# Half of w2 in parts for the second group's later experts, and attention units that share their TensorE stretches

## The chip, the cores and the metric

The kernel runs on one core of one Trainium2 chip. The metric is the device time of one execution in microseconds, as the median over several runs; lower is better. Before the change it is 1072.7 us (three runs, 1072.57 to 1072.9).

## The reference

An attention block feeds a mixture of experts. B=4 batches, H=8 heads, S=768 positions, D=48 per head; then N=3072 rows of 384 features, E=4 experts, F=1024 hidden units, all in float32.

```python
for t in range(S):                      # gated linear attention, recurrent form
    state = alpha[:, :, t, :, None] * state + einsum('bhd,bhe->bhde', k[:, :, t], v[:, :, t])
    y[:, :, t] = einsum('bhd,bhde->bhe', q[:, :, t], state)
x = y.transpose(0, 2, 1, 3).reshape(B * S, H * D)
p = domain_probs / (domain_probs.sum(-1, keepdims=True) + 1e-09)
for e in range(E):
    h = maximum(x @ w1[e], 0.0)
    out += p[:, e:e + 1] * (h @ w2[e])
```

## The kernel before

**Attention in units.** The sequence is cut into chunks of 128 positions, 6 chunks for each of 4 batches. That makes 24 units, numbered `u`, chunk by chunk; unit `u` works on all 8 heads of one batch and one chunk. `attention(u)` is a generator with 17 steps:

- Steps 0 to 2 transpose alpha, keys and queries on TensorE (`tp`) and ask for the next unit's alpha, keys and queries from memory.
- The chunk is treated in 7 levels of doubling block length. Each level copies a part of the queries (`copy_q`, ScalarE, tile `qb`), multiplies the queries with decays (`next_q`, VectorE) and the keys too (`next_k`, both). Each level needs the one before it. Steps 3 to 6 are levels 0 to 2 and the query copy of level 3.
- Step 7 multiplies queries and keys for levels 0 to 3 on TensorE (`products`, tile `sc`, 64 records) and merges them under masks (`take`). Steps 8, 9 and 10 are levels 4, 5 and 6.
- Step 11 is `far` (the last level) and the products of levels 4 and 5 (`sc`, 32 records). Steps 12 and 13 copy the scores to the tile `lat`, step 14 transposes the keys back.
- Step 15 is `result()`: it multiplies scores with values and queries with the state (tile `yps`). Step 16 is the state update: a product of keys and values (tile `sps`), two VectorE operations for each half of the state, and the loads of the values of unit `u + 2`. Of the product `sps` only the blocks of a head with itself are used.

**Experts in groups.** The 24 units are put in 7 groups: the first of 2 units, five of 4, the last of 2. A group of 4 gives 512 rows of x. A task is one group with one expert; the last two groups share each expert's weights. `up(gi, e, fc)` computes one of 8 row tiles of h (128 hidden units x 512 rows) into the PSUM tiles `one` and `two`; `down(gi, e, slots, between)` multiplies h with w2 for one or two of the group's units into `ops`, and `add_up` adds that to the accumulator `acc`, weighted by the expert's probability.

**Products in parts.** A float32 product on TensorE can be done plainly, or as three products of the type float32r with operands split into `top`, `low` and a correction `dif`. `split1(gi, e)` and `split2(gi, e)` say which task has w1 or w2 in parts: w1 from the second group on, w2 from the third. In parts, h is split too (`hidden_parts`: a ScalarE relu, a VectorE operation for `low`, two half-width ones for `dif`); plainly, it is a relu in place (`rectified`). The `up` sets VectorE `t<-t,two` or `hT<-t,two` accordingly.

**Splitting the weights.** The first group splits w1 and the second group splits w2, each weight in 16 pieces (4 per expert). `split_piece` takes two ScalarE operations and two VectorE operations per piece, in steps that `background()` runs between other work, and a GpSimd DMA writes the split piece to a buffer in memory (`kept`), from where later groups load it (SyncE queue). The second group's raw w2 piece is loaded into a part of the h tile that is free, and `down` uses it plainly from there.

**Who sets the order.** Everything is put out in an order written by hand: `advance(cost)` moves a clock by a nominal cost for every row tile of an `up` and for every product of a `down`, and runs the attention steps whose time has come. `deal()` gives these times: unit `u` ends at a due time before its group is wanted, `space` apart from its neighbours, and lasts twice `space`, so that two units overlap. The steps' places within a unit are the list `BEATS`:

```python
BEATS = [*(0.055 * (j + 1) for j in range(11)), 0.69, 0.75, 0.8, 0.87, 0.94, 1.0]
...
begin = max(end - 2 * space, ends[-2])
events += [(begin + (end - begin) * beat, u, run) for beat in BEATS]
```

[...] `one`, `two` and `ops` share four PSUM banks (tag `g`), the transposes, `yps` and `sps` two (tag `w`), the scores two (tag `sc`).

Of the kernel before, what the change touches and what calls it, by code (L numbers as in the profile page):

```python
# [10 lines left out]
F32 = mybir.dt.float32  # L11
# [9 lines left out]
def kernel(  # L21
# [122 lines left out]
    accs = {}  # L144


    BEATS = [*(0.055 * (j + 1) for j in range(11)), 0.69, 0.75, 0.8, 0.87, 0.94, 1.0]
    MARGIN = 6.0
    waiting = deque()
    clock = 0.0  # L150
# [1 line left out]


    split1 = lambda gi, e: gi > 0
    split2 = lambda gi, e: gi > 1
    makes = [lambda gi, e: gi == 0, lambda gi, e: gi == 1]


# [28 lines left out]
    def load_piece(l, i, beside=False):  # L187
        if i >= E * NQ * LAST:
            return
        gi, k = divmod(i, E * NQ)  # L190
        e, c = divmod(k, NQ)
        if (split1, split2)[l](gi, e):
            w = wt[l][i] = wts.tile([P, 3, KC * QF], F32R, name=f"w{l + 1}",
                                    bufs=AHEAD if l == 0 else NQ)
            nc.sync.dma_start(out=w.bitcast(F32), in_=kept[l][k])
            return
        if l == 1 and not beside:
            return
        if l == 0:

            if gi > 0 or e == 0:
                shared[c] = wts.tile([P, 3, KC * QF], F32R, name="w2", bufs=NQ)
            w = shared[c][:, 2 - e % 2 if gi == 0 else 2].bitcast(F32)
        else:

            w = hidden[c][:, 0].rearrange("p f n -> p (f n)")[:, :KC * QF].bitcast(F32)
        wt[l][i] = w
        if l == 0:
            heads = moe_w1[e].rearrange("(h d) f -> h d f", d=D)[:, :, c * QF:(c + 1) * QF]
            w = w.rearrange("p (c f) -> p c f", f=QF)  # L210
            for part in range(2):
                nc.sync.dma_start(out=w[:, part], in_=heads[part * H // 2:(part + 1) * H // 2, :QUAD])
            nc.sync.dma_start(out=w[:, 2], in_=heads[:, QUAD:])
        else:
            nc.sync.dma_start(
                out=w.rearrange("p (c d) -> p c d", d=DM),
                in_=moe_w2[e].rearrange("(c p) d -> p c d", p=P)[:, c * FPQ:(c + 1) * FPQ])

    def split_piece(l, i):
        whole = wt[l][i]  # L220
        w = wts.tile([P, 3, KC * QF], F32R, name=f"w{l + 1}", bufs=AHEAD if l == 0 else NQ)
        top, low, dif = (w[:, part] for part in range(3))

        nc.scalar.activation(out=top, in_=whole, func=ACT.Copy, scale=TRIM)
        yield
        nc.scalar.activation(out=dif, in_=whole, func=ACT.Copy, scale=TRIM * 4096)
        yield
        nc.vector.scalar_tensor_tensor(out=low, in0=whole, scalar=4096.0, in1=dif.bitcast(F32),
                                       op0=ALU.mult, op1=ALU.subtract)
        nc.vector.tensor_sub(dif, low.bitcast(F32), top.bitcast(F32))  # L230
        nc.gpsimd.dma_start(out=kept[l][i % (E * NQ)], in_=w.bitcast(F32))
        if l == 0:
            del wt[0][i]

    def background():

# [32 lines left out]
    def attention(u):  # L269
# [41 lines left out]
        def next_q(li):  # L311
            m = LEVELS[li]
            qv = halves(QT, m)[:, :, :, 1, :]
            dv = halved(decs[li])
            nc.vector.tensor_mul(qv, qv, spread(dv[:, :, :, 0], m))  # L315
            dec = work.tile([P, NP, P // (2 * m)], F32, name=f"dec{li}", bufs=1)
            nc.vector.tensor_mul(dec, dv[:, :, :, 0], dv[:, :, :, 1])
            decs.append(dec)

# [138 lines left out]

        if cb < NCB - 1:
            KB = AT  # L460
            sps = ps.tile([P, NP, 2, D], F32, name="sps", tag="w")
            for p in range(NP):
                nc.tensor.matmul(sps[:, p], lhsT=KB[:, p, :], rhs=rv[:, 2 * p:2 * p + 2, :D],  # L463
                                 start=True, stop=True)
            for i in range(2):
                rows = slice(HD * i, HD * (i + 1))
                old, add = st[rows, :, i, :], sps[rows, :, i, :]
# [35 lines left out]
    def up(gi, e, fc, slots=None):  # L503
# [8 lines left out]
        if fc in ((0, 2) if gi == 1 else (0,)) and begins and not split2(gi, e):  # L512
            half = range(fc, fc + 2) if gi == 1 else range(NQ)
            for k in half:
                load_piece(1, (gi * E + e) * NQ + k, beside=True)
        if makes[0](gi, e) and ends and fc in SPLIT_AT[e in (0, E - 1)]:
            k = SPLIT_AT[e in (0, E - 1)].index(fc)
            making.append(split_piece(0, (gi * E + e) * NQ + k))
# [16 lines left out]
        else:  # L535
# [16 lines left out]
            if split2(gi, e):  # L552
# [44 lines left out]
    def down(gi, e, slots, between):  # L597
# [2 lines left out]
        first = first_piece(gi, e)  # L600
        halves_ = split2(gi, e)
        if slots[0] == 0 and makes[1](gi, e):
            making.extend(split_piece(1, first + k) for k in range(NQ))
        if slots[0] == 0 and makes[0](gi, e) and 0 < e < E - 1:
            making.extend(split_piece(0, first + k) for k in range(2, NQ))
        sums = [[ps.tile([P, DM], F32, name=f"ops{j}", tag="g", bufs=4)
                 for j in range(2 if halves_ else 1)] for _ in slots]

        kinds = [((0, 1), range(FCH - 2)), ((0, 1), range(FCH - 2, FCH)), ((2,), range(FCH))]
        steps = [(part, i, fc) for parts, tiles in (kinds if halves_ else [((3,), range(FCH))])  # L610
                 for part in parts for i in range(len(slots)) for fc in tiles]
        for n, (part, i, fc) in enumerate(steps):
            c, f = divmod(fc, FPQ)
            h = hidden[c][:, :, f, slots[i] * P:(slots[i] + 1) * P]
            advance(cost(1, gi, e) / FCH / (3 if halves_ else 1))
# [6 lines left out]
            if halves_:  # L622
                w = wt[1][first + c].rearrange("p t (c d) -> p t c d", d=DM)[:, part, f]
                nc.tensor.matmul(sums[i][part // 2], lhsT=h[:, part], rhs=w,  # L624
                                 start=(fc == 0 and part != 1), stop=(fc == FCH - 1 and part != 0))
            else:
                w = wt[1][first + c].rearrange("p (c d) -> p c d", d=DM)[:, f]
                nc.tensor.matmul(sums[i][0], lhsT=h[:, 2].bitcast(F32), rhs=w,  # L628
                                 start=(fc == 0), stop=(fc == FCH - 1))
            if part >= 1 and fc == FCH - 1:  # L630
                add_up(gi, e, slots[i], part // 2, sums[i][part // 2 if halves_ else 0])
        while between:
            between.popleft()[1]()
        background()
# [35 lines left out]
    def cost(layer, gi, e):  # L670
        n = len(groups[gi]) / 4
        if layer == 0:
            return 2.1 * n if split1(gi, e) else 2.6 * n
        return 4.1 if split2(gi, e) else 5.4

    def deal():

# [2 lines left out]
        wanted = [0.0]  # L680
        ends = [0.0, 0.0]
        events = []
        t = 0.0
        for (gi, e), after in zip(tasks, tasks[1:]):
            part = 1 - 1 / len(groups[0]) if gi == e == 0 else 1
# [122 lines left out]
```

## Time and profile before

| | |
|---|---|
| median of 3 runs | 1072.7 us (1072.57 to 1072.9) |
| profiled execution | 1073.32 us, span 1071.6 us |
| TensorE clock granted, mean | 0.998 |
| TensorE busy | 1048.1 us, 98% |
| VectorE busy | 775.2 us, 72% |
| ScalarE busy | 566.7 us, 53% |
| DMA | 251.67 MB, mean 235 GB/s |

In the profile PE is TensorE, PEld its weight loads, DVE VectorE, ACT ScalarE, POOL GpSimd and SP SyncE. L624 is line 624 of the kernel. A timeline line gives the start and the length in us of a run of like instructions, the engine, the line and the operation, what is written and read with the shape, the number of records in it, and in brackets the idle time before it. The shape 128*64 is a stationary operand of 128 rows and 64 columns, 128x512 the moving operand. A float32 product that is done plainly shows as two records, one in float32r as one. A line of the waits has who waited for whom, the total us, the number of times and the longest. In the windows each engine's busy us stand with its number of instructions.

The second group's up and down phases lie between 165 and 352 us, with an up of an expert at 216 and a down at 237, for example. The third group starts its ups at 352. The last attention unit ends at about 872 us, and after that only expert work is left.

### The profile page before, as it was taken

What the parts mean: (1) busy time and instruction counts of PE and PEld (TensorE: products, weight loads), DVE (VectorE), ACT (ScalarE), POOL (GpSimd) and SP (SyncE); (2) the same over time, 40 slices, a digit from 0 to 9 for tenths busy, and PEclk for the clock granted to TensorE, in tenths of its full rate; (3) what the DMA queues carried; (4) which work ended last, traced back from release to release, by engine and by line L of the source; (5) the groups of instructions that cost most, each with busy time, mean ns of one, the idle gap of its engine ahead of it and who ended that gap; (6) DMA issues with size and microseconds to landing.
All of it is one profiled execution on the core that took longest, in us unless ns stands there. A gap on an engine that the chain in (4) does not pass through costs nothing.

```text
span 1071.6 us, 21614 instructions
## 1 busy us (share of the span) xinstructions
PE 1048.1 (98%) x8460; PEld 899.1 (84%) x8460; DVE 775.2 (72%) x1711; ACT 566.7 (53%) x1202; POOL 32.7 (3%) x71
## 2 busy tenths in 40 slices
PE   8899999999999999999999999999999999999998
PEld 8777777676776798898898898898889889898988
DVE  5488776656566978778877777986787866666565
ACT  5687866575656554536546445555464543323232
POOL 2010000000000100000000000000000000000000
PEclk9999999999999999999999999999999999999999
DMA  8597699687696967758759558586594543544540
GB/s 123 156 330 216 230 328 368 238 328 241 236 309 209 402 216 274 281 160 312 268 170 359 204 187 337 186 281 234 158 358 173 221 192 147 207 177 178 187 181 31
DMA packets 158838, 251.67 MB, mean 235 GB/s; under 512 B 120112, under 2 KB 135344, under 8 KB 136208
## 3 DMA queue, kind: packets, MB, share of 16 engines
q1 hardware_dynamic: 149600, 208.82, 57.1%
q0 software_dynamic: 5760, 41.29, 9.8%
q8 instruction: 67, 1.10, 0.4%
q10 hardware_dynamic: 3376, 0.17, 0.3%
q14 instruction: 35, 0.29, 0.1%
HBM read 207.79 MB, written 42.47 MB: 234 GB/s over the span
## 4 chain that ended last, share of the span: by engine, by line
PE 83%; DVE 8%; ACT 6%; issue 2%; DMA 1%; SPq 0%; DVEq 0%; ACTq 0%
PE ops L624 25%; PE one L540 21%; PE ops L628 10%; PE two L540 10%; PE sc L334 6%; PE yps L428 3%; PE tp L266 3%; PE one L532 2%; ACT qb L308 2%; PE far L389 1%; PE sps L463 1%; DVE near L344 1%; DVE t L553 1%; DVE hT L580 1%; DVE hT L590 1%
## 5 line engine op out<-in xcount | busy, mean ns | idle before, releaser
L624 PE MATMUL ops<-w,hT 128*128 128x384 f32 x1728 | 318.0, 339 | 4.4 <-DVE acc L658 4.3
L624 PEld LDWEIGHTS ops<-w,hT 128*128 128x128 f32 x1728 | 299.1, 188 | 9.9 <-DVE acc L658 5.6
L540 PE MATMUL one<-xT,w 128*128 128x512 f32 x960 | 253.8, 400 | 2.6 <-DVE xT L248 1.1
L540 PEld LDWEIGHTS one<-xT,w 128*128 128x128 f32 x960 | 176.3, 188 | 41.8 <-DVE QT L315 1.6
L551 ACT ACTIVATE t<-one 128x512 f32<-128x512 f32 (+1 forms) x192 | 106.3, 554 | 153.6 <-PE one L540 148.5
L308 ACT COPY qb<-QT 64x256 f32<-64x256 f32 x336 | 136.4, 406 | 77.0 <-DVE QT L289 44.1
L578 ACT ACTIVATE hT<-t 128x512 fp32r<-128x512 f32 (+1 forms) x160 | 94.3, 589 | 123.6 <-DVE t L553 122.9
L580 DVE SCALAR_TENSOR_TENSOR hT<-t,hT 128x512 fp32r<-128x512 f32 (+1 forms) x160 | 102.2, 638 | 55.7 <-ACT hT L578 53.6
L540 PE MATMUL two<-xT,w 128*128 128x512 f32 x480 | 136.7, 393 | 0.0
L628 PE MATMUL ops<-hT 128*128 128x384 f32 x384 | 133.4, 491 | 0.0
L553 DVE TENSOR_TENSOR t<-t,two 128x512 f32<-128x512 f32 (+1 forms) x160 | 100.8, 630 | 41.9 <-ACT t L551 21.4
L590 DVE SCALAR_TENSOR_TENSOR hT<-hT 128x256 fp32r<-128x256 f32 x288 | 111.9, 422 | 4.4
L540 PEld LDWEIGHTS two<-xT,w 128*128 128x128 f32 x480 | 90.6, 189 | 20.0
L628 PEld LDWEIGHTS ops<-hT 128*128 128x128 f32 x384 | 69.5, 190 | 40.1 <-issue 0.4
L315 DVE TENSOR_TENSOR QT<-QT,dec 128x256 f32<-128x256 f32 x144 | 60.8, 422 | 38.2 <-ACT qb L308 37.5
L344 DVE COPY_PREDICATED near<-masks,sc 128x256 f32<-128x256 uint8 x144 | 77.0, 535 | 15.5 <-PE sc L334 12.8
L334 PEld LDWEIGHTS sc<-qb,KT 128*64 128x64 f32 x2304 | 72.7, 138 | 9.7 <-issue 5.6
L334 PE MATMUL sc<-qb,KT 128*64 128x64 f32 x2304 | 77.2, 223 | 2.6 <-ACT qb L308 2.6
L658 DVE SCALAR_TENSOR_TENSOR acc<-ops,p_all,acc 128x384 f32<-128x384 f32 x82 | 49.5, 614 | 33.9 <-PE ops L624 14.5
L326 ACT COPY KT<-KT 128x256 f32<-128x256 f32 x144 | 59.9, 416 | 3.2
L327 DVE TENSOR_TENSOR KT<-KT,dec 128x256 f32<-128x256 f32 x144 | 60.3, 419 | 0.0
L558 DVE TENSOR_TENSOR hT<-t,two 128x512 f32<-128x512 f32 x32 | 22.0, 688 | 35.6 <-ACT t L551 23.0
(88 smaller groups left out, 970.7 us busy)
## 6 DMA issues: line engine op xcount, KB each, us to landing
w<-kept SPq DMA_DIRECT2D x144, 1152.0 KB
kept<-w POOLq DMA_DIRECT2D x32, 1152.0 KB, 7.4
hT<-in_moe_w_dram SPq DMA_DIRECT2D x32, 384.0 KB
w<-in_moe_w_dram SPq DMA_DIRECT2D x48, 128.0 KB
ra<-in_alpha_dram SPq DMA_DIRECT2D x23, 192.0 KB
rk<-in_k_dram SPq DMA_DIRECT2D x23, 192.0 KB
rq<-in_q_dram SPq DMA_DIRECT2D x23, 192.0 KB
out_dram<-acc POOLq DMA_DIRECT2D x18, 192.0 KB, 6.6
```

What stands on the lines that cost most here:

```text
L308: nc.scalar.copy(out=qb[rows, :, i, :].rearrange("p a (b r) -> p a b r", r=m), in_=qv[rows])
L315: nc.vector.tensor_mul(qv, qv, spread(dv[:, :, :, 0], m))
L334: nc.tensor.matmul(out[HALF * s:HALF * (s + 1), 2 * p:2 * p + 2, :], lhsT=KTs[li][:, p, HALF * s:HALF * (s + 1)], rhs=qbs[li][:, p, :, QUA ...
L344: nc.vector.copy_predicated(near.rearrange("p a (b two r) -> p a b two r", two=2, r=m)[:, :, :, 1, :], mk.unsqueeze(1).broadcast_to([P, H, ...
L540: nc.tensor.matmul(out, lhsT=w[:, part, kc], rhs=x_part(gi, part, kc), start=(part == terms[0] and kc == 0), stop=(part == terms[-1] and k ...
L551: nc.scalar.activation(out=t, in_=one, func=ACT.Copy, scale=FINE)
L553: nc.vector.tensor_add(t, t, two)
L578: nc.scalar.activation(out=top, in_=x, func=ACT.Relu, scale=TRIM)
L580: nc.vector.scalar_tensor_tensor(out=low, in0=x, scalar=0.0, in1=top.bitcast(F32), op0=ALU.max, op1=ALU.subtract)
L590: nc.vector.scalar_tensor_tensor(out=dif, in0=top.bitcast(F32), scalar=1 / 4096.0, in1=low.bitcast(F32), op0=ALU.mult, op1=ALU.subtract)
L624: nc.tensor.matmul(sums[i][part // 2], lhsT=h[:, part], rhs=w, start=(fc == 0 and part != 1), stop=(fc == FCH - 1 and part != 0))
L628: nc.tensor.matmul(sums[i][0], lhsT=h[:, 2].bitcast(F32), rhs=w, start=(fc == 0), stop=(fc == FCH - 1))
```

## The change

It has two parts.

**w2 in parts.** For the second group (`gi == 1`), experts 1 to 3, the first two of the four w2 pieces are used in parts: `split2` takes the piece number. Their raw loads go to a free part of another h tile (`hidden[c + 2][:, 1]`), the splits are put into the up after its row tiles 2 and 4 instead of into the down, and the split tile stays in use until the down has read it. The down of these tasks takes two units at a time and adds up in two sums each: the parts `top` and `low` of row tiles 0 to 3, then the plain products of row tiles 4 to 7, then `dif` of row tiles 0 to 3. The nominal cost of such a product is 4.7 instead of 5.4 per unit.

**Attention units that share stretches.** From unit 10 on (`pairs_from`, the fourth group's first) the steps' places are the list `IN_PAIRS`, in which the steps up to 11 come earlier and the last at 1.02. `TOGETHER` then sets step 7 of a unit to the very time of step 15 of the unit before, and step 11 to that of step 16, if the two are nearer than a sixth of `space`; the steps between are spread evenly. The state update of units 9 to 19 is done with one 64-column product per head instead of one 128-column product per pair of heads, so that only the used blocks are computed. One decay tile gets a second buffer. The units of the fourth and fifth groups are dealt from 6 nominal us earlier on (`MARGIN`), which makes their spacing equal to one expert's nominal time.

```diff
+    IN_PAIRS = [*(0.0425 * (j + 1) for j in range(8)), 0.385, 0.43, 0.475, 0.52, 0.6, 0.67, 0.755, 0.84, 1.02]
+    TOGETHER = ((15, 7), (16, 11))
+    pairs_from = half + 2 * B
...
-    split2 = lambda gi, e: gi > 1
+    split2 = lambda gi, e, c=0: gi > 1 or gi == 1 and e > 0 and c < NQ // 2
...
-            w = hidden[c][:, 0].rearrange("p f n -> p (f n)")[:, :KC * QF].bitcast(F32)
+            place = (hidden[c][:, 0] if not split2(gi, e, c) else hidden[c + NQ // 2][:, 1])
+            w = place.rearrange("p f n -> p (f n)")[:, :KC * QF].bitcast(F32)
...
+        elif split2(1, *divmod(i - E * NQ, NQ)):
+            wt[1][i] = w
...
-            dec = work.tile([P, NP, P // (2 * m)], F32, name=f"dec{li}", bufs=1)
+            dec = work.tile([P, NP, P // (2 * m)], F32, name=f"dec{li}", bufs=1 + (li == 6))
...
-            sps = ps.tile([P, NP, 2, D], F32, name="sps", tag="w")
+            apart_ = u + 1 >= pairs_from
+            sps = ps.tile([P, NP, 1 if apart_ else 2, D], F32, name="sps", tag="w")
             for p in range(NP):
-                nc.tensor.matmul(sps[:, p], lhsT=KB[:, p, :], rhs=rv[:, 2 * p:2 * p + 2, :D],
-                                 start=True, stop=True)
+                for i in range(2) if apart_ else [slice(0, 2)]:
+                    rows = slice(HD * i, HD * (i + 1)) if apart_ else slice(0, P)
+                    nc.tensor.matmul(
+                        sps[rows, p], lhsT=KB[:, p, rows],
+                        rhs=rv[:, 2 * p + i, :D] if apart_ else rv[:, 2 * p:2 * p + 2, :D],
+                        start=True, stop=True)
...
+        if gi == 1 and e > 0 and fc in (2, 4):
+            making.append(split_piece(1, first_piece(gi, e) + fc // 2 - 1))
...
-            making.extend(split_piece(1, first + k) for k in range(NQ))
+            making.extend(split_piece(1, first + k) for k in range(NQ // 2 if halves_ else 0, NQ))
...
+        if not halves_:
+            kinds = [((3,), range(FCH))]
+        elif gi == 1:
+
+            kinds = [((0, 1), range(FCH // 2)), ((3,), range(FCH // 2, FCH)), ((2,), range(FCH // 2))]
...
-        return 4.1 if split2(gi, e) else 5.4
+        return 4.1 if gi > 1 else 4.7 if split2(gi, e) else 5.4
...
-            first = wanted[gi - 1] if gi > 1 else 0.0
+            first = wanted[gi - 1] - MARGIN * (2 < gi < LAST - 1) if gi > 1 else 0.0
...
-                events += [(begin + (end - begin) * beat, u, run) for beat in BEATS]
+                pairs = u >= pairs_from
+                beats = [0.0, *(IN_PAIRS if pairs else BEATS)]
+                due_at = {-1: begin, **{j: begin + (end - begin) * beats[j + 1] for j in (7, 11, 16)}}
+                for ahead, j in TOGETHER if pairs else ():
+                    if (u > pairs_from or j == 11) and abs(times[-1][ahead] - due_at[j]) < space / 6:
+                        due_at[j] = times[-1][ahead]
```

The second hunk of `split2`'s users (loads, the start and stop flags of the down's products, `add_up`) follows from these.

More of the change, by code (lines that the diff above doesn't have):

```diff
@@ L191, in load_piece @@
         e, c = divmod(k, NQ)
-        if (split1, split2)[l](gi, e):
+        if gi > l:
             w = wt[l][i] = wts.tile([P, 3, KC * QF], F32R, name=f"w{l + 1}",
@@ L460, in attention @@
             KB = AT
-            sps = ps.tile([P, NP, 2, D], F32, name="sps", tag="w")
+            apart_ = u + 1 >= pairs_from
+            sps = ps.tile([P, NP, 1 if apart_ else 2, D], F32, name="sps", tag="w")
             for p in range(NP):
-                nc.tensor.matmul(sps[:, p], lhsT=KB[:, p, :], rhs=rv[:, 2 * p:2 * p + 2, :D],
-                                 start=True, stop=True)
+                for i in range(2) if apart_ else [slice(0, 2)]:
[4 more added lines that the diff above has]
+                        start=True, stop=True)
             for i in range(2):
                 rows = slice(HD * i, HD * (i + 1))
-                old, add = st[rows, :, i, :], sps[rows, :, i, :]
+                old, add = st[rows, :, i, :], sps[rows, :, 0 if apart_ else i, :]
                 if cb == 0:
@@ L511, in up @@
                 hidden[k] = hid.tile([P, 3, FPQ, NT], F32R, name="hT", bufs=NQ)
-        if fc in ((0, 2) if gi == 1 else (0,)) and begins and not split2(gi, e):
+        if fc in ((0, 2) if gi == 1 else (0,)) and begins and gi < 2:
             half = range(fc, fc + 2) if gi == 1 else range(NQ)
@@ L551, in up @@
             nc.scalar.activation(out=t, in_=one, func=ACT.Copy, scale=FINE)
-            if split2(gi, e):
+            if split2(gi, e, c):
                 nc.vector.tensor_add(t, t, two)
@@ L609, in down @@
         kinds = [((0, 1), range(FCH - 2)), ((0, 1), range(FCH - 2, FCH)), ((2,), range(FCH))]
-        steps = [(part, i, fc) for parts, tiles in (kinds if halves_ else [((3,), range(FCH))])
+        if not halves_:
+            kinds = [((3,), range(FCH))]
+        elif gi == 1:
+            kinds = [((0, 1), range(FCH // 2)), ((3,), range(FCH // 2, FCH)), ((2,), range(FCH // 2))]
+        steps = [(part, i, fc) for parts, tiles in kinds
                  for part in parts for i in range(len(slots)) for fc in tiles]
+        sides = [[s for s, step in enumerate(steps) if (step[0] // 2 if halves_ else 0, step[1]) == key]
+                 for key in ((side, i) for i in range(len(slots)) for side in range(len(sums[0])))]
+        firsts, lasts = {s[0] for s in sides}, {s[-1] for s in sides}
         for n, (part, i, fc) in enumerate(steps):
@@ L614, in down @@
             h = hidden[c][:, :, f, slots[i] * P:(slots[i] + 1) * P]
-            advance(cost(1, gi, e) / FCH / (3 if halves_ else 1))
+            advance(cost(1, gi, e) * len(slots) / len(steps))
             while between and n >= between[0][0] * len(steps):
@@ L621, in down @@
                 make_dif(*later.popleft())
-            if halves_:
+            side = part // 2 if halves_ else 0
+            if part < 3:
                 w = wt[1][first + c].rearrange("p t (c d) -> p t c d", d=DM)[:, part, f]
-                nc.tensor.matmul(sums[i][part // 2], lhsT=h[:, part], rhs=w,
-                                 start=(fc == 0 and part != 1), stop=(fc == FCH - 1 and part != 0))
+                h = h[:, part]
             else:
                 w = wt[1][first + c].rearrange("p (c d) -> p c d", d=DM)[:, f]
[L628 to L631, printed above, removed]
+                h = h[:, 2].bitcast(F32)
+            nc.tensor.matmul(sums[i][side], lhsT=h, rhs=w, start=(n in firsts), stop=(n in lasts))
+            if n in lasts:
+                add_up(gi, e, slots[i], part // 2, sums[i][side])
         while between:
@@ L682, in deal @@
         events = []
+        times = []
         t = 0.0
@@ L703, in deal @@
                 run = attention(u)
-                events += [(begin + (end - begin) * beat, u, run) for beat in BEATS]
+                pairs = u >= pairs_from
[4 more added lines that the diff above has]
+                        due_at[j] = times[-1][ahead]
+                marks = sorted(due_at)
+                times.append([])
+                for lo, hi in zip(marks, marks[1:]):
+                    times[-1] += [due_at[hi] if j == hi else
+                                  due_at[lo] + (due_at[hi] - due_at[lo]) * (beats[j + 1] - beats[lo + 1])
+                                  / (beats[hi + 1] - beats[lo + 1]) for j in range(lo + 1, hi + 1)]
+                events += [(time, u, run) for time in times[-1]]
         return sorted(events, key=lambda x: x[:2])
```

## The prediction

> **What bounds the kernel now.** I read the page first, then the timeline of TensorE (PE) in one expert of the second group and one of the fourth, then the windows by stage, then the waits.
>
> ```profile
> PE 1048.1 (98%) x8460; PEld 899.1 (84%) x8460; DVE 775.2 (72%) x1711; ACT 566.7 (53%) x1202; POOL 32.7 (3%) x71
> PE 83%; DVE 8%; ACT 6%; issue 2%; DMA 1%; SPq 0%; DVEq 0%; ACTq 0%
> ```
>
> PE is busy nearly everywhere and is 83% of the chain. Work taken off PE is time gained, as long as the waits do not grow. So the question is what PE's instructions cost start to start (a start is exact, an end is modelled).
>
> ```profile
> 244.16 3.39 PE L628 MATMUL ops<-hT 128*128 128x384 f32 x10
> 247.39 0.60 PE L266 MATMUL tp<-ident,rk 128*128 128x128 f32 x4
> 247.83 4.04 PE L628 MATMUL ops<-hT 128*128 128x384 f32 x12
> 251.70 0.60 PE L266 MATMUL tp<-ident,rq 128*128 128x128 f32 x4
> ...
> 613.52 0.85 PE L540 MATMUL two<-xT,w 128*128 128x512 f32 x3
> 614.30 0.43 PE L428 MATMUL yps<-QT,st 128*32 128x128 f32 x8
> ...
> 615.97 2.09 PE L334 MATMUL sc<-qb,KT 128*64 128x64 f32 x64
> 617.98 1.67 PE L540 MATMUL one<-xT,w 128*128 128x512 f32 x6
> 619.49 0.85 PE L540 MATMUL two<-xT,w 128*128 128x512 f32 x3
> 620.18 1.02 PE L463 MATMUL sps<-rv,AT 128*128 128x96 f32 x8
> 620.99 1.63 PE L540 MATMUL one<-xT,w 128*128 128x512 f32 x6
> ...
> 625.20 7.86 PE L624 MATMUL ops<-w,hT 128*128 128x384 f32 x44
> 632.99 0.66 PE L389 MATMUL far<-qb,KT 128*64 128x128 f32 x8
> 633.47 1.10 PE L334 MATMUL sc<-qb,KT 128*64 128x64 f32 x32
> 634.50 2.21 PE L624 MATMUL ops<-w,hT 128*128 128x384 f32 x11
> ```
>
> From these starts: a plain record of L628 takes (251.70 - 247.83) / 12 = 0.323 us, and a product is two records (384 records for 192 products), 0.646. A record in parts (L624) takes 0.174 (7.79 for 44, less the switch below); a product is three, 0.522. The state update takes 620.99 - 620.18 = 0.81 for its 8 records. 32 score records cost 2.01 - 1.03 = 0.98, so 16 cost 0.49. The starts also show what entering the narrow column forms (128*64, 128*32) costs: the last gap before is 268 ns instead of 174 after L624, 416 instead of 323 after L628; leaving costs about 100 ns more. yps and sc already stand side by side here: one entry and one exit for both.
>
> ```profile
> 216.00:234.00 18.00, 18.00 (x104) 14.56 (x103) 8.62 (x18) 15.16 (x32) 0.00 (x0) 1.00 1.00 389
> 234.00:261.00 27.00, 27.00 (x225) 18.02 (x222) 20.34 (x43) 14.70 (x29) 2.12 (x4) 1.00 0.65 211
> 393.00:413.00 20.00, 20.00 (x200) 16.93 (x200) 14.74 (x31) 11.86 (x24) 0.00 (x0) 1.00 0.91 362
> 413.00:435.00 22.00, 22.00 (x158) 21.03 (x157) 18.86 (x47) 10.76 (x24) 0.00 (x0) 1.00 0.48 138
> ```
>
> The columns after the length are PE, weight loads, DVE, ACT, POOL, clock, DMA share, GB/s. The first pair is the up and the down of an expert of the second group, the second pair of the third group. PE is full in all four; in the third group DVE stands at 74% and 86% and PE still runs through.
>
> ```profile
> PEld far L389 <- ACT qb L308: 4.3, 3, 2.2
> PE ops L624 <- DVE acc L658: 4.3, 4, 1.9
> ```
>
> These are the two waits that the change can feed: `far` waiting for the last query copy, and a down waiting for DVE. Both are small now.
>
> [...] The 128-column records of the state update and the transposes start 108 to 112 ns apart; in the 64-column scores two records share 60 ns. [...]
>
> **The change, part by part.** The sum is against the profiled span, 1071.6; that execution took 1073.3, the median run 1072.7. I apply the difference to the median.
>
> *w2 in parts.* 4 row tiles x 4 slots x 3 experts = 48 plain products become three records each: 48 x (0.646 - 0.522) = 5.95 us less on PE, which is the bound there. Added on DVE: 12 row tiles x (0.693 + 2 x 0.422) = 18.4 and 12 more accumulations x 0.612 = 7.3. ACT does the same relu into another form. Two of an expert's four splits (2 x 0.95 DVE each) move from the down to the up. By stage, DVE in the up goes to 8.6 + 4 x 1.115 + 3.8 = 17 of 21 us, in the down to 20.3 - 3.8 + 1.7 + 2.4 = 21 of 25: 80 to 85%, which the third group carries without PE stalls. The early split is behind row tile 2, some 6 us after the up begins; its raw load is issued at the end of the down before (the trace has it at 258 for an up that begins at 261), so ACT should find it landed. Behind it on ACT is the eviction of `one`, for which PE would wait. SP's next loads are held until the previous w2 hidden piece is free, about 2 us later than now; they are w1 pieces for the next expert, 40 us ahead. POOL writes two of the kept pieces in the up (DMA share already 0.9 to 1.0): nothing on PE reads those before the third group. The third group's first two w2 loads now wait for the end of the last down, about 20 us before use. I take +0.4 for this, from -0.3 (some waits go) to +3.
>
> *State update in 64-column form, beside `far`.* Units 9 to 19 have it, 11 units. 16 records of 64 stationary columns cost 0.49 at the scores' rate (bounds 0.36 for 48 moving columns of 64, and 0.81, no gain) against 0.81. Where it stands directly ahead of the next unit's `far` it adds no switch: 0.32 gained. I worked out deal()'s times: spacing is 33.2, the update falls at 1.02 x 66.4, the next unit's `far` at 0.52 x 66.4 after a start 33.2 later, and both get one time; only at unit 18, where the spacing drops to 26.7, the distance is 5.8 against the limit 4.45 and they stay apart (0.13 gained). 10 x 0.32 + 0.13 = 3.3. *Scores with the result*: L428 then L334 adjacent is already so for 11 of the 13 units 11 to 23 in the trace; unit 14 joins: 0.2. Together 3.5.
>
> *Moved steps.* The levels' copies come at 0.0425 instead of 0.055 of 66.4; step 10 (last query copy) to step 11 (`far`) shrinks from 5.4 nominal to 3.0. The v loads stay with the update, the a, k, q loads come a few us earlier; each has a unit's spacing of slack on SP, so nothing. The gain of regular spacing is also a risk: relative to a down's start every unit of groups 4 and 5 now falls alike, scores after the first row tile of the up, `far` after the sixth. I followed ACT and DVE through that up by hand with the row means (add 0.68, relu 0.63, low 0.69, half dif 0.42, evictions 0.59, query copies 0.81). The last query copy is ready 16.75 us after the up's start and PE comes to `far`, behind the update, at 16.7: a wait of 0 to 0.3, I take 0.1 for 14 units, 1.4. DVE ends the up 5.5 us behind PE against 4.7 in the up of 603 to 625; the down needs the last relu after 24 records, 4.2 us, with 0.2 to spare now: 0.3 for 8 experts, 2.4. Against that, old waits of 0.26, 0.64 and 0.66 (at 459, 593, 677) go: -1.6. Bounds: everything hidden, -1.6; or 1 us at each of 22 places, +22.
>
> Sum: -5.95 - 3.5 + 0.4 + 1.4 + 2.4 - 1.6 = -6.9. Span 1064.7, median 1065.8.
>
> **Rivals.**
> *All hidden.* The new waits stay at nothing: -5.95 - 3.5 - 1.6 = -11.0, 1061.7. For it: PE now has no gap over 0.3 us from 216 to 458. Against: `far` has only 0.1 to 3 us to spare in units 11, 12, 13, 17 and 19 with today's wider spacing.
> *The second group gives its gain back.* The early split waits for its raw piece or for ACT, and the down for it: 6 pieces x 1 us, 1071.8, no change. For it: DMA share 1.00 in that up, with writes added. Against: some 6 to 9 us between issue and need.
> *Slower: the compressed levels.* Each level is a chain of ACT copy (0.81) and DVE product (0.42) that needs the one before; with 3.0 us steps and DVE at full load, the copy falls behind, and PE stands at L389 for L308, then the down at L658. It decides from 12 us of new waits, 0.85 a unit over 14 units; at 1 us per unit plus 0.3 per expert it would be 1065.8 - 3.8 + 14 + 1.5 = 1077. For it: unit 19 waits already, and compressing takes 3 us from `far`. Against: if I subtract that from each unit's slack now and add the update's 0.5 ahead of it, twelve of the fourteen keep 0.1 us or more.
> *Not what it says.* If the times do not meet within a sixth of the spacing, each update pays its own entry and exit: 11 x 0.13 = 1.4 instead of 3.5, 1067.9, inside the likeliest case.
>
> **Numbers.** Likeliest case 0.62 (own range 1062.5 to 1070.3), all hidden 0.15, gain given back 0.11, slower 0.12. About 0.2% (2.1 us) is what a measurement of this kernel can tell from no change, so faster means below 1070.5. The likeliest gives 0.60 to faster, 0.02 to no change; all hidden 0.15 to faster; given back 0.02, 0.08, 0.01; slower 0.02 to no change and 0.10 to slower: 0.77, 0.12, 0.11. The range takes 1060.5 to 1074.0; outside stay the worst of the slower case and gains beyond my sum.
>
> **What would show it.** The plain records (ops<-hT) fall from 384 to 288, those in parts (ops<-w,hT) rise by 144; the ups and downs of experts 1 to 3 of the second group shorten by 2 us each. The state update shows 128*64 records in 0.5 us directly ahead of `far`, ten times. Right on the waits: L389 for L308 stays under 3 us, waits of L624 under 4. Wrong if the second group does not shorten by 5 to 6 us, or if those two waits pass 8 us together.

## The result and the profile after

The changed kernel takes 1079.9 us (four runs, 1079.1 to 1082.3) against 1072.75 us for the kernel before on the same chip: a ratio of 1.0070 (95% interval 1.0053 to 1.0088). It is slower by about 7 us, where 1065.8 was forecast and 1074.0 was the upper end of the range. The profiled execution took 1082.25 us (span 1080.5, mean clock 0.995). Executions of one program differ by some 3 us with the stretches at half clock that they happen to have: of 43 executions of the kernel before, beside later experiments, the 13 with a mean clock of 1.000 took 1071.9 us on average, the 17 with 0.998 took 1073.5 and the seven with 0.996 took 1075.1.

Most helper lines moved: L624 and L628 are now L652, L540 is L555, L389 is L397, L308 is L316, L463 is L474, L658 is L681, and the VectorE lines of the hidden rows are L568, L595 and L605. These are the answering lines of the page: TensorE's row, the chain by engine, and the two groups of w2 records.

```profile
PE 1045.4 (97%) x8596; PEld 901.7 (83%) x8596; DVE 795.0 (74%) x1759; ACT 567.7 (53%) x1202; POOL 32.8 (3%) x71
PE 67%; DVE 18%; ACT 7%; issue 4%; DMA 3%; SPq 1%; DVEq 0%; ACTq 0%
L652 PE MATMUL ops<-w,hT 128*128 128x384 f32 x1872 | 348.3, 342 | 5.9 <-DVE acc L681 5.1
L652 PE MATMUL ops<-hT 128*128 128x384 f32 x288 | 100.6, 491 | 0.0
```

The plain records are 288, those in parts 1872: the change does what it says. PE's busy time went down by 2.7 us while the span went up by 8.9. The loss is therefore waiting, and the chain says on whom: DVE has 18% of it where it had 8%, PE 67% where it had 83%.

The narrow state update is also as described. This is PE's timeline in an up of the third group:

```profile
366.22 0.67 PE L474 MATMUL sps<-rv,AT 128*64 128x48 f32 x16
366.73 0.62 PE L397 MATMUL far<-qb,KT 128*64 128x128 f32 x8
```

Sixteen records take 0.51 us from start to start, directly ahead of `far`, without an entry of their own.

Now the waits of PE in the third and fourth groups alone (352 to 698 us), the kernel before first, then the changed one. Each line has the total, the number of times and the longest.

```profile
PE ops L624 <- DVE acc L658: 1.0, 2, 0.5
```

```profile
PE far L397 <- DVE hT L595: 5.0, 1, 5.0
PE ops L652 <- DVE acc L681: 4.7, 7, 1.7
PE ops L652 <- ACT acc L679: 0.6, 2, 0.4
```

One microsecond became ten. Two things are to be seen: one single wait of 5.0 us, and seven waits of a down for VectorE's `add_up` (two more go to ScalarE's L679).

**Where the single wait is.** The timeline of the changed kernel around it; unit 18 stands at its step 11, and brackets hold the idle time before a line:

```profile
670.30 1.20 PE L652 MATMUL ops<-w,hT 128*128 128x384 f32 x6
...
672.60 0.42 DVE L323 TENSOR_TENSOR QT<-QT,dec 128x256 f32<-128x256 f32 x1
...
674.45 0.68 DVE L568 TENSOR_TENSOR t<-t,two 128x512 f32<-128x512 f32 x1
675.16 0.63 ACT L593 ACTIVATE hT<-t 128x512 fp32r<-128x512 f32 x1 [1.33 <-DVE t L568]
675.70 0.80 ACT L316 COPY qb<-QT 64x256 f32<-64x256 f32 x2
...
676.55 1.12 PE L397 MATMUL far<-qb,KT 128*64 128x128 f32 x8 [5.04 <-DVE hT L595]
```

The bracket names DVE's L595, but `far` starts when the query copy of L316 ends. That copy was held in ScalarE's order behind the relu of the last row tile (L593), and that relu waited for VectorE's addition (L568), which was still working off the up. VectorE had the queries ready at 673.0 (L323); ScalarE still did two instructions of the up (L566 and L593) before the copy, with 1.33 us of standing still ahead of the second, and began the copy at 675.7. A down had begun with six records; `far` came after them in the order and PE stood.

**What follows it.** A window of the changed kernel around the end of the wait (busy us of PE, PEld, DVE, ACT, POOL with counts, then clock, DMA share, GB/s):

```profile
674.80:681.60 6.80, 5.05 (x47) 4.93 (x48) 4.33 (x13) 3.00 (x6) 0.00 (x0) 0.50 0.04 16
```

For 6.8 us the clock is half: PE ran dry at 671.5, the clock fell at 674.8 and was full again at 681.6. The w2 records in it start 320 ns apart (679.8 to 681.4), against 174 at full clock. PE was busy for 5.05 us of these 6.8, so an estimate of half of that, some 2.5 us, was lost on top of the wait.

**Where the seven waits are.** The longest, in the changed kernel's timeline:

```profile
418.92 7.18 PE L652 MATMUL ops<-w,hT 128*128 128x384 f32 x40
422.14 0.55 DVE L293 TENSOR_TENSOR t<-rq,rk 128x384 f32<-128x384 f32 x1
...
424.47 1.43 DVE L605 SCALAR_TENSOR_TENSOR hT<-hT 128x256 fp32r<-128x256 f32 x4
...
427.15 0.62 DVE L681 SCALAR_TENSOR_TENSOR acc<-ops,p_fine,acc 128x384 f32<-128x384 f32 x1
427.82 2.03 PE L652 MATMUL ops<-w,hT 128*128 128x384 f32 x10 [1.71 <-DVE acc L681]
```

The first 48 records of the down are done at about 426.1. The next pair of units needs a PSUM bank that `add_up` (L681) has to free, and VectorE comes to it a microsecond late: it still has the halves of `dif` (L605) from the up, and between them the first levels of the next attention unit.

### The profile page after: what moved, and what is told of

Read it like the earlier page. It is cut to its first block, busy times and chain, and to the rows that moved or that the text cites. A ratio compares the mean times of both kernels' runs of the same rounds, so it can differ in the third digit from the quotient of the medians.

```text
span 1080.5 us, 21961 instructions
## 1 busy us (share of the span) xinstructions
PE 1045.4 (97%) x8596; PEld 901.7 (83%) x8596; DVE 795.0 (74%) x1759; ACT 567.7 (53%) x1202; POOL 32.8 (3%) x71
## 4 chain that ended last, share of the span: by engine, by line
PE 67%; DVE 18%; ACT 7%; issue 4%; DMA 3%; SPq 1%; DVEq 0%; ACTq 0%
PE ops L652 30%; PE one L555 16%; PE two L555 8%; PE sc L342 4%; DVE t L568 4%; DVE hT L595 4%; PE yps L436 3%; ACT hT L593 2%; DVE near L352 2%; PE tp L274 2%; ACT qb L316 2%; PE one L547 2%; DMA rv<-in_v_dram 2%; DVE hT L605 2%; DMA rq<-in_q_dram 1%
## 5 line engine op out<-in xcount | busy, mean ns | idle before, releaser
L652 PE MATMUL ops<-w,hT 128*128 128x384 f32 x1872 | 348.3, 342 | 5.9 <-DVE acc L681 5.1
L652 PEld LDWEIGHTS ops<-w,hT 128*128 128x128 f32 x1872 | 323.6, 189 | 13.6 <-DVE acc L681 7.6
L555 PE MATMUL one<-xT,w 128*128 128x512 f32 x960 | 255.4, 401 | 1.9 <-DVE xT L256 1.2
L555 PEld LDWEIGHTS one<-xT,w 128*128 128x128 f32 x960 | 177.3, 188 | 44.0 <-DVE xT L256 1.9
L566 ACT ACTIVATE t<-one 128x512 f32<-128x512 f32 (+1 forms) x192 | 106.2, 553 | 147.8 <-PE one L555 143.1
L593 ACT ACTIVATE hT<-t 128x512 fp32r<-128x512 f32 (+1 forms) x172 | 101.8, 592 | 142.7 <-DVE t L568 142.1
L316 ACT COPY qb<-QT 64x256 f32<-64x256 f32 x336 | 136.6, 407 | 53.1 <-DVE QT L297 23.6
L595 DVE SCALAR_TENSOR_TENSOR hT<-t,hT 128x512 fp32r<-128x512 f32 (+1 forms) x172 | 110.3, 641 | 56.6 <-ACT hT L593 55.5
L568 DVE TENSOR_TENSOR t<-t,two 128x512 f32<-128x512 f32 (+1 forms) x172 | 108.9, 633 | 46.1 <-PE two L555 27.7
L555 PE MATMUL two<-xT,w 128*128 128x512 f32 x480 | 138.5, 396 | 0.0
L605 DVE SCALAR_TENSOR_TENSOR hT<-hT 128x256 fp32r<-128x256 f32 x312 | 121.8, 422 | 4.8
L555 PEld LDWEIGHTS two<-xT,w 128*128 128x128 f32 x480 | 90.5, 189 | 22.1 <-DVE t L568 0.2
L652 PE MATMUL ops<-hT 128*128 128x384 f32 x288 | 100.6, 491 | 0.0
L323 DVE TENSOR_TENSOR QT<-QT,dec 128x256 f32<-128x256 f32 x144 | 60.7, 421 | 38.8 <-ACT qb L316 38.3
L652 PEld LDWEIGHTS ops<-hT 128*128 128x128 f32 x288 | 52.1, 190 | 29.0 <-issue 0.4
L681 DVE SCALAR_TENSOR_TENSOR acc<-ops,p_all,acc 128x384 f32<-128x384 f32 x82 | 49.8, 615 | 28.0 <-PE ops L652 21.5
L681 DVE SCALAR_TENSOR_TENSOR acc<-ops,p_fine,acc 128x384 f32<-128x384 f32 x60 | 36.0, 612 | 23.6 <-PE ops L652 23.5
```

Of the source, the lines that this page charges most:

```text
L316: nc.scalar.copy(out=qb[rows, :, i, :].rearrange("p a (b r) -> p a b r", r=m), in_=qv[rows])
L555: nc.tensor.matmul(out, lhsT=w[:, part, kc], rhs=x_part(gi, part, kc), start=(part == terms[0] and kc == 0), stop=(part == terms[-1] and k ...
L593: nc.scalar.activation(out=top, in_=x, func=ACT.Relu, scale=TRIM)
L595: nc.vector.scalar_tensor_tensor(out=low, in0=x, scalar=0.0, in1=top.bitcast(F32), op0=ALU.max, op1=ALU.subtract)
L605: nc.vector.scalar_tensor_tensor(out=dif, in0=top.bitcast(F32), scalar=1 / 4096.0, in1=low.bitcast(F32), op0=ALU.mult, op1=ALU.subtract)
L652: nc.tensor.matmul(sums[i][side], lhsT=h, rhs=w, start=(n in firsts), stop=(n in lasts))
```

## The experiments

Each kernel ran beside the kernel before on its chip; the ratio is to that. Line numbers are those of the changed kernel unless said.

### First: the two parts, and unit 18

**w2 in parts alone.**

```diff
-    pairs_from = half + 2 * B
+    pairs_from = len(units) + 1
-            first = wanted[gi - 1] - MARGIN * (2 < gi < LAST - 1) if gi > 1 else 0.0
+            first = wanted[gi - 1] if gi > 1 else 0.0
```

> The w2 half alone: split2, the early splits and the two-unit downs of the change, while every attention unit keeps the old steps (BEATS, 128-column state update, old spacing). Theory A (the loss sits in the attention half, mostly at unit 18's step 11, where TensorE waits 5.0 us for the query copy and then runs 6.8 us at half clock): the w2 half keeps most of its 5.95 us, so 1066.5 to 1069. Rival B (the second group gives its gain back through VectorE and the shifted attention): 1072 to 1075. In the trace A expects experts 1 to 3 of the second group about 2 us shorter each.

Measured: 1071.8 us, ratio 0.9978 (0.9969 to 0.9987). A gain, but only 2.4 us, less than Theory A expected.

**The attention part alone.**

```diff
-    split2 = lambda gi, e, c=0: gi > 1 or gi == 1 and e > 0 and c < NQ // 2
+    split2 = lambda gi, e, c=0: gi > 1
-        if gi == 1 and e > 0 and fc in (2, 4):
+        if split2(1, e) and gi == 1 and fc in (2, 4):
```

> The attention half alone: second group's w2 plain as before, units from 10 on with the new steps, the joint times and the 64-column state update. Theory A: the whole loss is here and the w2 gain is missing, so 1072.75 + 7.2 + 5 = about 1084 (1081 to 1086). Rival B: 1075 to 1078. If the wait of unit 18's step 11 depends on how deal's times fall after the second group's cost, it can also be smaller here; then the trace shows it.

This kernel's output is not right, for a reason that was not found, so only its time counts. Measured: 1083.0 us, ratio 1.0091 (1.0076 to 1.0106). Unit 18's wait is there with 5.1 us, and again 6.8 us at half clock behind it. So the loss comes with the attention part; the second buffer of a decay tile, treated below, is still in both of these kernels.

**Pairs only up to unit 17.**

```diff
-                pairs = u >= pairs_from
+                pairs = pairs_from <= u < 18
```

> The changed kernel, but units 18 to 23 take the old steps (BEATS) again; units 10 to 17 stay as changed. Theory A: the 5.0 us wait at unit 18, the 3.4 us that the half clock costs and the 2.2 us at unit 23 go, some old waits of units 19 to 23 (2 to 4 us) come back: 1072 to 1075. Rival C (the loss is in the regular part, the waits of the down for the accumulator in units 10 to 17, about 5 us): at least 1077.

Measured: 1079.3 us, ratio 1.0056 (1.0040 to 1.0073). Unit 18's wait is gone, but in the later units three downs wait for `add_up` (1.6, 1.8 and 1.6 us), with 3.4 us at half clock behind the second, at 768. That missed the number of Theory A and lies in the range of Rival C, but it decides nothing on unit 18, since it moves every later unit too.

**Unit 18's step 11 alone, 5 nominal us later.**

```diff
+                if u == 18:
+                    due_at[11] += 5.0
```

> The changed kernel with a single time moved: step 11 of unit 18 falls due 5 nominal us later, inside the down instead of at its start. Theory A: the 5.0 us wait and with it the half clock go, 1071.5 to 1075. Rival C: no more than 1 to 2 us better, 1078 to 1079.

Measured: 1076.5 us, ratio 1.0028 (1.0017 to 1.0039), 0.42% below the changed kernel's ratio, 4.5 us. PE's timeline of this kernel at the same place:

```profile
670.55 1.65 PE L652 MATMUL ops<-w,hT 128*128 128x384 f32 x8 [1.25 <-DVE t L568]
...
677.10 0.66 PE L397 MATMUL far<-qb,KT 128*64 128x128 f32 x8 [0.35 <-ACT qb L316]
```

With other records of the down ahead of `far`, the wait splits into 1.25 and 0.35, and no half clock follows (mean clock of this execution 1.000). The single wait is thus more than half of the loss, but not all: without it the kernel is still slower than before, and the time lies between the ranges of the two theories.

### Second: the second buffer of one decay tile

In the traces a 512-column record of an up took 233.5 ns from start to start in the changed kernel and in the four above, 229.6 before. What they have in common is the second buffer of the last decay tile (`dec6`). It takes 32 bytes per partition, and it moves the tiles placed after it by as much: `xT` (in the programs as built, from byte 147424 to 147456), the hidden tile, the raw x and the accumulator.

**That buffer alone, in the kernel before.**

```diff
-            dec = work.tile([P, NP, P // (2 * m)], F32, name=f"dec{li}", bufs=1)
+            dec = work.tile([P, NP, P // (2 * m)], F32, name=f"dec{li}", bufs=1 + (li == 6))
```

> The kernel before with one line of the change alone: the decay tile dec6 gets its second buffer. No instruction changes; the tiles that are placed behind it in SBUF (xT, x_raw, hT, acc) move by 32 bytes per partition. Theory D (the placement costs TensorE time): the records of the ups go from 229.6 to 233.5 ns apart as in the changed kernel, 1440 x 3.9 ns less 0.6 us in the downs, so about 5 us slower, 1077 to 1079. Rival (the 3.9 ns come with something else of the change, or with the chip): no change, 1072 to 1074.

Measured: 1076.5 us, ratio 1.0040 (1.0028 to 1.0052). The same instructions cost 4 us more, a little less than Theory D expected. PE's timeline in one of the last ups, without attention beside it, first the kernel before, then this one (whose lines have the same numbers):

```profile
914.62 1.54 PE L540 MATMUL one<-xT,w 128*128 128x512 f32 x6
...
931.10 1.14 PE L624 MATMUL ops<-w,hT 128*128 128x384 f32 x5
```

```profile
917.29 1.57 PE L540 MATMUL one<-xT,w 128*128 128x512 f32 x6
...
934.09 1.22 PE L624 MATMUL ops<-w,hT 128*128 128x384 f32 x6
```

72 records take 16.48 us before (229 ns) and 16.80 here (233 ns), with no wait in either. The kernel has 1440 such records: 1440 x 3.9 ns = 5.6 us, less 0.6 ns on each of the records in parts (174.6 to 174.0), 1.0 us, comes near the 4.0 measured.

**A third buffer, in the changed kernel** (64 bytes from the old place).

```diff
-            dec = work.tile([P, NP, P // (2 * m)], F32, name=f"dec{li}", bufs=1 + (li == 6))
+            dec = work.tile([P, NP, P // (2 * m)], F32, name=f"dec{li}", bufs=1 + 2 * (li == 6))
```

> The changed kernel with a third buffer for dec6, which nothing uses: xT and hT move by another 32 bytes, so that they lie 64 bytes from their places before. Theory D in the form that 64 bytes are the period: up records back at 229.6 ns, about 5 us faster than the changed kernel, 1074 to 1076. If the period is longer, they stay at 233 and the time at 1079 to 1081. Without D: 1079 to 1081 too, and then the run of the second buffer alone decides.

Measured: 1083.7 us, ratio 1.0101 (1.0087 to 1.0114); the records of the ups take 232.6 ns. They aren't back, so a period of 64 bytes is not the reason; that theory fell. The time is above both ranges, because here the records in parts of the downs, which read the hidden tile, take 175.9 ns against 173.9 in the changed kernel: 1872 x 2.0 ns = 3.7 us more, less 1440 x 0.9 ns = 1.3 us in the ups, which gives 2.4 of the 3.3 us (0.31%) between the two kernels.

**The same with unit 18's step 11 later** (both edits above).

> Both repairs on the changed kernel: the third buffer of dec6 and step 11 of unit 18 due 5 nominal us later. If the two causes are independent they add: about 5 us from the placement and 3 to 5 from the wait at unit 18 below the changed kernel's 1079.9, so 1070 to 1072. If the placement does nothing: 1075 to 1077, as with unit 18 alone.

Measured: 1078.3 us, ratio 1.0053 (1.0038 to 1.0068), above both ranges, because the third buffer costs time where it was hoped to gain some. Unit 18's edit again takes 0.48%.

**w2 in parts alone, with one buffer** (the first experiment with `bufs=1`).

> The w2 half alone, with dec6 in one buffer as before, so that xT and hT lie where they lay. Theory D: the w2 half is worth what the prediction gave it, 4.5 to 6 us, so 1067 to 1068.5, against the 2.3 us measured with the second buffer. Rival (the w2 half itself loses more than half of its gain): 1070 to 1071.

Measured: 1069.6 us, ratio 0.9967 (0.9954 to 0.9980): 3.5 us faster than before, between the ranges of the theory and the rival.

**The changed kernel with the second buffer in another pool**, where it moves neither `xT` nor the hidden tile.

```diff
+            other = li == 6 and u % 2
-            dec = work.tile([P, NP, P // (2 * m)], F32, name=f"dec{li}", bufs=1 + (li == 6))
+            dec = (hid if other else work).tile([P, NP, P // (2 * m)], F32,
+                                                name=f"dec{li}" + "b" * other, bufs=1)
```

> The changed kernel, with the second dec6 buffer taken from another pool (units of odd number use it), so that xT, x_raw and hT lie exactly where they lay before; acc alone moves by 32 bytes. Theory D (placement): up records at 229.6 ns instead of 233.5, 3 to 5 us faster than the changed kernel, 1075 to 1077. Rival: the records stay at 233.5 and the time at 1079 to 1081.

Measured: 1079.7 us, ratio 1.0060 (1.0045 to 1.0075). The up records are back at 229.6 ns though the accumulator alone is still moved, so the accumulator's place is not what slows them. Yet the kernel is only 0.1% faster than the changed one, 1 us where 3 to 5 were expected, and that is not clear of zero. In the third and fourth groups it takes 341.9 us against 342.2, and the waits of the downs there are 0.9 us longer together (7.7 us against 6.8, start to start). That fits a reading in which a faster up only comes to the wait sooner. In the second group PE waits 1.9 us before a transpose at 285 us (1.8 at 288 in the changed kernel), and here 3.4 us at half clock follow, which the changed kernel's trace doesn't have: that expert takes 47.4 us against 45.7. The rest was not followed up.

### Third: when the units are dealt

**All attention of the fourth and fifth groups' units 12 nominal us later**, on top of the last kernel; if the waits come from where the units fall in a down, they must go.

```diff
-            gi, due = gis[0], wanted[gis[-1]] - MARGIN
+            gi, due = gis[0], wanted[gis[-1]] - MARGIN * (-1 if 2 < gis[0] < LAST - 1 else 1)
-            first = wanted[gi - 1] - MARGIN * (2 < gi < LAST - 1) if gi > 1 else 0.0
+            first = wanted[gi - 1] + MARGIN * (gi > 2) if gi > 1 else 0.0
```

> As the kernel with dec6 elsewhere, and the units of the fourth and fifth groups are due 12 nominal us later, the first of the sixth group follow: steps 11 and 16 then fall into the middle of a down instead of the end of an up, steps 1 to 3 to its end, and unit 18 meets unit 17 by itself. Theory E (TensorE waits in the middle of the downs for L681 because the levels 4 to 6, the update and the next unit's first steps all fall between the end of the up and the first half of the down): these waits, 6.8 us in the third and fourth groups, fall under 2, unit 18's goes, and the time is 1064 to 1069. Rival F (the accumulator's waits come from the 64-column form or from the regular pairing itself, wherever it falls): 1071 to 1076.

Measured: 1071.7 us, ratio 0.9983 (0.9975 to 0.9991). By its time alone this is Rival F's range; the trace shows that the waits of Theory E went and others came. The waits view of this kernel lists only these for PE between 352 and 698 us:

```profile
PE ops L654 <- DMA w<-kept: 0.7, 1, 0.7
PE one L557 <- DVE acc L683: 0.5, 1, 0.5
```

No down waits for `add_up` in this stretch any more (L654 is L652 of the changed kernel, L683 its L681, L399 its L397), and unit 18's wait is gone. The third and fourth groups take 331.8 us against 341.9. But the last units now wait; the timeline near the end of the attention:

```profile
838.70 1.66 ACT L513 ACTIVATE xT<-x_raw 128x512 fp32r<-128x512 f32 x3
840.27 0.80 ACT L316 COPY qb<-QT 64x256 f32<-64x256 f32 x2
841.12 1.12 PE L399 MATMUL far<-qb,KT 128*64 128x128 f32 x8 [4.87 <-ACT qb L316]
```

The query copy is late behind ScalarE's split of x this time, and PE again pays 4.9 us and 6.8 us of half clock, with one more wait, of a down for VectorE, of 2.6 us at 754 and 3.4 us of half clock behind that:

```profile
754.43 0.69 PE L654 MATMUL ops<-w,hT 128*128 128x384 f32 x1 [2.63 <-DVE acc L683]
```

```profile
754.10:757.50 3.40, 3.07 (x49) 2.56 (x53) 3.40 (x9) 0.00 (x0) 0.00 (x0) 0.51 0.02 5
```

The fifth group takes 181.6 us against 171.9.

**Second buffer elsewhere and unit 18's step 11 later** (both edits above).

> As the kernel with dec6 elsewhere, and step 11 of unit 18 due 5 nominal us later, all other times as in the change. The waits in the downs of the third and fourth groups stay (about 6 us). If placement and unit 18 are independent: 1071 to 1073. The distance to the kernel with everything 12 later is the price of where the pairs fall.

Measured: 1074.4 us, ratio 1.0011 (1.0004 to 1.0019), 0.49% or 5.3 us below the same kernel without the edit at unit 18, and somewhat above the range. The kernel with everything 12 later is only 0.28% below it; that is not the price of where the pairs fall, since the later one pays for its new waits at 754 and 841 us.

**Later, and the last units as before**: on top of the kernel dealt later, the shift of the last groups' start undone and the old places (`BEATS`) from unit 18 on.

```diff
-            first = wanted[gi - 1] + MARGIN * (gi > 2) if gi > 1 else 0.0
+            first = wanted[gi - 1] + MARGIN * (2 < gi < LAST - 1) if gi > 1 else 0.0
-                pairs = u >= pairs_from
+                pairs = pairs_from <= u < 18
```

> As the kernel with everything 12 later, but units 18 to 23 take the old steps at the old spacing. Theory G (what that kernel still loses is one thing: step 11 of units 21 to 23 falls into the first quarter of a down, where ScalarE and VectorE are a row tile and more behind): the last third of the attention returns from 181.5 to about 174 us, the waits of 4.9, 2.8 and 1.2 us and their half clock go, and the time is 1064 to 1067, below both kernels. Rival H (the compressed steps are not to blame, the last units wait wherever they fall once the units before are dealt later): 1069 to 1072.

Measured: 1064.3 us (1062.5 to 1066.1), ratio 0.9906 (0.9891 to 0.9920): faster than both kernels, within the range of Theory G, and below the 1065.8 that was forecast for the change. Its chain by engine on the page:

```profile
PE 80%; DVE 7%; DMA 5%; ACT 5%; issue 2%; SPq 1%; DVEq 0%; ACTq 0%
```

It has as many instructions on PE, DVE and ACT as the changed kernel (8596, 1759 and 1202). DVE's share of the chain falls from 18% to 7%. What differs is the order, and the place of the second buffer.

The stages in the profiled executions, one of each kernel, in us. "w2 alone" is the kernel with one buffer; "elsewhere" and "later, last old" are the second buffer's other pool and the kernel just shown. In the changed kernel one result with its scores, 3.7 us, moved from the third group into the second, so these two cells are to be read together.

| stage | before | w2 alone | changed | elsewhere | later, last old |
|---|---|---|---|---|---|
| second group, experts 1 to 3 | 136.5 | 131.8 | 137.5 | 138.8 | 131.3 |
| third and fourth groups | 335.4 | 335.0 | 342.2 | 341.9 | 331.8 |
| fifth group | 174.3 | 174.1 | 172.2 | 171.9 | 175.1 |

## Why the prediction was wrong

By ratios, the 0.70% come apart so, in the order in which the experiments take them off (parts in us, rounded; each is a ratio of two measured kernels, uncertain by 0.13 to 0.23 points):

| term | in the sum | measured |
|---|---|---|
| w2 in parts (0.9967) | -5.5 | -3.5 |
| narrow update | -3.3 | -3.3 (by its records) |
| other moved steps (1.0011 over 0.9967, the update taken out; the sum's 0.2 for scores included) | +2.0 | +8.0 |
| unit 18's wait (1.0060 over 1.0011) | 0 | +5.3 |
| moved tiles (1.0070 over 1.0060) | 0 | +1, not clear of zero |

The steps that failed are thus the waits: the term for the moved steps was 6 us too small, and unit 18's wait was put at nothing.

**w2 in parts: the mechanism right, the size too large.** In its own stage the profile gives 136.5 - 131.8 = 4.7, a little short of the 5 to 6 us that the prediction named as its sign, and the timed runs 3.5 (interval 2.1 to 4.9), with the forecast of 5.5 outside. Where the rest went was not traced. In the kernel with w2 alone VectorE has 144.1 busy us in the 187 us from 165 on, where it had 117.2 before, and no down of the second group waits for it: the longest wait of a down there is 0.4 us, for ScalarE. So most of the gain stayed. The rival "gives its gain back" is excluded as long as attention isn't moved.

**The narrow update: right.** From start to start the eleven updates take 5.6 us instead of 8.9, 3.3 less, and ten of them stand directly ahead of `far`, as forecast. The scores beside the result (0.2 in the sum) were not measured by themselves. No switch was left to pay ten times, so "not what it says" falls.

**Unit 18: the step that failed first.** The prediction worked out that the two steps stay apart there, credited only 0.13 us for its update, and put a wait there at nothing. What it did not ask is where step 11 then stands: just behind the start of a down, when ScalarE and VectorE still have the up's last row tiles ahead of the query copy. Three pairs of kernels that differ in this one time alone put it at 4.5 to 5.3 us, wait and half clock together.

**The waits on VectorE: right in kind, wrong in place and size.** The prediction followed ACT and DVE by hand through an up and took the last relu as the point where a down would wait, +2.4, less 1.6 for old waits. In the up its working held: `far` came without a noticeable wait in the regular units. The waits are further on, in the middle of the down, where the second pair of units needs a bank that `add_up` frees. From start to start the nine waits of the downs in the third and fourth groups come to 6.8 us, against two of 1.3 us before. They recur because all units of these groups now fall alike relative to a down. That the fixed place is the cause is shown by dealing the units 12 nominal us later, which removes all of them with the same instructions; which single VectorE operation would have to move was not tried. One further wait, before a transpose at 288 us in the second group, 1.8 us in the changed kernel and gone in the later-dealt one, was not priced either. These two, 5.5 and 1.8 us more, make up most of the 8.0; the rest was not split up.

**The second buffer: not seen at all.** The prediction has no term for the buffer, since it looked at instructions and waits and not at where tiles lie. Alone it costs 4 us; in the changed kernel 1 us was measured, with intervals that overlap almost wholly. In w2 alone, one buffer against two is 0.9967 against 0.9978, whose intervals overlap too, so that its size beside other changes is open, between nothing and some 3 us.

**The rivals.** "Slower: the compressed levels" named the two right waits and that they feed each other, but spread them over 14 units at about 1 us, and had 12% of the chance. In truth the regular units were nearly just in time, as the prediction's slack had it, and the loss sat in one irregular unit and in the downs. The test that the prediction set for itself, the two waits above 8 us together, failed clearly: over the whole span the view of waits has 10.1 us for `far` (5.1 in three waits for the query copy, and the 5.0 of unit 18) and 5.1 for the down, 15 together, where the same view had 3.1 and 4.3 before (the 4.3 that the prediction reads for `far` is the line of its weight loads, PEld).

**What stays open.** Why the place of a tile changes the pace of a record, and which one does it. Of the moved tiles the records of the ups read `xT` and those of the downs the hidden tile, but the two always moved together with the raw x; only the accumulator is ruled out.

## What to carry to other kernels

When steps are put at a fixed place in a repeating schedule, follow every queue through the whole period, down as well as up, and look hardest at the one unit that doesn't fit the pattern: here it cost some 5 us, more than the 3.3 us that the narrow updates of all units gained. Before giving up a change that saves work and loses time, shift its phase; with the second buffer in the other pool in both, the steps dealt 12 nominal us later, with the last units left at their old places, turned +0.6% into -0.9%. And compare the pace of a record in a stretch without waits: here a change of 4 ns there came from moved tiles and not from the order.

## What the runs showed of the hardware

- The pace of the records changed with the place of the tiles behind the decay tile. With these moved by 0 bytes (the kernel before), 32 (the same with a second buffer) and 64 (the changed kernel with a third), the 512-column records of the ups took 229.6, 233.5 and 232.6 ns, and the 384-column records in parts of the downs 174.6, 174.0 and 175.9 ns, in stretches without waits.
- A stall of 5.0 us at unit 18 was followed by 6.8 us at half clock, one of 5.3 us at the same place, with the second buffer elsewhere, by 3.4. In the first the estimate above, 2.5 us, is half of the wait's own length.
- After shorter stalls both were seen: 3.4 us at half clock followed 1.8 us (at 768 us with pairs up to unit 17), 1.9 (at 285 us, second buffer elsewhere), 2.2 (at 756 us in the last kernel) and 2.6 us (at 754 us in the kernel dealt later); none followed 1.9 us at 765 us in the kernel before or 2.1 us at 853 us in the changed one. So the length of the stall alone does not sort these cases.
- The stretches between changes of the clock in the middle of the changed kernel's trace are 163.8 us full, 3.4 half, 501.8 full, 6.8 half and 399.4 full, which are 48, 1, 147, 2 and 117 times 3.413; in that of the kernel before they are 160.4 full, 3.4 half and 901.1 full, 47, 1 and 264 times. In the last 3.4 us ahead of the half clock PE was busy for 1.28 us in the kernel before (at 164.0 us), and for 1.54 (at 166.2) and 0.12 us (at 671.4) in the changed one (ends of PE records are modelled). Why one stall of some 2 us is followed by half clock and another is not, was not shown.
